# A kernel-made instruction order for most of the first expert layer, with retention decays and part of the weight splits moved from GpSimd to VectorE

## The chip, the cores and the metric

The kernel runs on one NeuronCore of one Trainium2 chip. The metric is the device time of one execution in microseconds (us). The engines are named as the profile names them: PE is TensorE (matmuls), DVE is VectorE, ACT is ScalarE, POOL is GpSimd, SP is SyncE, whose queue issues all DMAs of this kernel.

## The reference

Retention (attention with a fixed decay per head and no softmax) feeds two dense layers one after the other; all is float32.

```python
batch, n_heads, seq, head_dim = (4, 8, 576, 64)      # 2304 tokens, d_model 512, d_ff 2048
scores = scale * np.matmul(q, k.transpose(0, 1, 3, 2))
Dmat = np.where(rel >= 0, gamma[:, None, None] ** rel[None, :, :], 0.0)
attn = np.matmul(scores * Dmat[None], v)
x = attn.transpose(0, 2, 1, 3).reshape(B * S, H * D)
h = x @ w_in;  g = h * np.cos(h);  x = g @ w_out                        # first layer
h = x @ w_in;  g = where(h >= 1, h, where(h <= -1, 0, (h + 1)**2 / 4)); out = g @ w_out   # second layer
```

## The kernel before

The weights arrive as float64 bit patterns, and the kernel turns them into float32 by integer and float operations on VectorE and ScalarE. Every matmul is done as three float32r products: each operand is split into a high part (a copy, on ScalarE) and a low part (the operand minus the high part, on VectorE or GpSimd).

The first layer works on five blocks of tokens (256, then four of 512), and for each block on 16 strips of 128 hidden units. One strip of one block is a **slot**; there are 80. A slot has these steps, named by letters in the code:

- `m`: 12 matmuls into a PSUM tile `h` (for the last block, in every second slot `bkS` or `bkO` instead);
- `a` on ScalarE and `A` on VectorE (L662, L666): reduce `h` to a turn, tile `t`;
- `b` on ScalarE (L670, L671): the cosine;
- `C` on VectorE (L675): times `h`, which frees the `h` tile;
- `g` on ScalarE (L683) and `G` on GpSimd (L688): high and low part, tiles `gh` and `gl`;
- `M`, two slots later: 12 matmuls into the four output banks `bky`; every third one reads `gl`.

There are two `h` tiles, so `m` of a slot waits for `C` of the slot two before it.

Three other things run beside the slots, from slot 28 on. First, the retention of the last nine pieces of a sequence (chunks of 64 or 128 tokens): load `qkv`, multiply by decay tables (`decay_q` L370, `decay_k` L380, on GpSimd), score matmuls, a mask on VectorE (tile `R`, L472), the attend matmuls that read `R`, the state `T`, and the high and low parts of the result (`xhl`). Second, the 32 pieces of the second layer's weights: load `raw`, ScalarE's `X`, VectorE's `W`, `X` and `V` (L239, L240, L275, L276), high and low part (`cw`, L291 and L292), sums of halves (`V`, L300 to L302), their parts (`tw`: L304 on ScalarE, and L306 on VectorE for one of the two matrices, L308 on GpSimd for the other), and stores to `wq` and `wv` in HBM. Third, reloads of the first layer's weights (`wi` from `wd`) for each slot from 32 on.

The engines run their instructions in a fixed order each. The opening and the whole second layer are put in order by the kernel: the opening by a written list, the second layer by a small planner, `listed`, which takes operations with a cost, a wanted position and the places that they read and write, runs the five engines through, and emits the operations in the order of the planned starts. Slots 24 to 79 are left to the framework's scheduler (`by_hand[0] = 0`): the loop below only says in which order they are written.

Of the kernel before, what the change touches and what calls it, by code (L numbers as in the profile page):

```python
# [20 lines left out]
P = 128  # L21
# [16 lines left out]
EARLY = (0, 2, 3, 1, 4)  # L38
XEARLY = {5: 6, 6: 8}
# [11 lines left out]
COST = dict(PE=1.04, mm2=2.72, psum=0.556, wide=0.96, copy=0.85, square=0.9, evac=0.68, pool=2.15, load=0.06)  # L51
LAG = 2
# [58 lines left out]
def retention_moe_kernel(ctx: ExitStack, tc: tile.TileContext, qk, kv, win1, wout1, win2, wout2, ktab, out):  # L111
# [169 lines left out]
    def spill(i, c, begun):  # L281
        q, second = c % NQ, c >= NQ
        if not second:
            half_w[i, q] = cv.tile([P, 2, DM], F32, tag="rsh", name="V")
        v = half_w[i, q][:, int(second), :]
        to_fp32(begun, v)
        t = wr.tile([P, 2, 2, 2 * P], F32R, tag="wi", name="cw")
        kept = ((((1, 0), (2, 1)), ((3, 1),)), (((1, 0),), ((2, 0), (3, 1))))[i][second]
        ks = slice(kept[0][1], kept[-1][1] + 1)
        u = v.rearrange("p (k m) -> p k m", k=2)[:, ks]  # L290
        A.activation(t[:, ks, 0], u, AF.Copy)  # L291
        V.tensor_tensor(out=t[:, ks, 1], in0=u, in1=f(t)[:, ks, 0], op=ALU.subtract)  # L292
        for p, k in kept:
            SY.dma_start(out=spilled(i, q, p), in_=f(t)[:, k])

    def spill_sums(i, q):

        v = half_w.pop((i, q)).rearrange("p s (k m) -> p (s k) m", k=2)
        firsts, seconds, v21 = ((v[:, 0::2], v[:, 2:4], v[:, 1]), (v[:, 0:2], v[:, 1::2], v[:, 2]))[i]
        V.tensor_tensor(out=firsts, in0=seconds, in1=firsts, op=ALU.subtract)  # L300
        V.tensor_tensor(out=v[:, 3], in0=v[:, 3], in1=v[:, 0], op=ALU.subtract)
        V.tensor_tensor(out=v21, in0=v21, in1=v[:, 3], op=ALU.subtract)  # L302
        t = xp.tile([P, 4, 2, 2 * P], F32R, tag="x", name="tw")
        A.activation(t[:, :, 0], v, AF.Copy)  # L304
        if i == 0:
            V.tensor_tensor(out=t[:, :, 1], in0=v, in1=f(t)[:, :, 0], op=ALU.subtract)  # L306
        for j in (0, 2)[:2 * i]:
            G.tensor_tensor(out=t[:, j:j + 2, 1], in0=v[:, j:j + 2], in1=f(t)[:, j:j + 2, 0], op=ALU.subtract)  # L308
        for j, p in enumerate(((5, 4, 7, 6), (5, 7, 4, 6))[i]):
            SY.dma_start(out=spilled(i, q, p), in_=f(t)[:, j])  # L310
# [320 lines left out]
    def copy_out(e, t, y, scale):  # L631
        if e % 2 == 0:
# [4 lines left out]
    def evac(s, home=None, only=None):  # L637
        l, c = slots[s]
        if c != NC - 1:
            return  # L640
        o, n = BLOCKS[l]
        per = 512 // n
        for e, y in enumerate(yb[l]):
            if only not in (None, e):
                continue
            t = stp.tile([P, 512], F32, tag="st", name="st") if home is None else home
            copy_out(e, t, y, -TWOPI)
            SY.dma_start(out=yd[:, e * per:(e + 1) * per, o:o + n], in_=t.rearrange("p (k n) -> p k n", k=per))
# [50 lines left out]
    plan = {}  # L699

    def at(pos, fn):
        plan.setdefault(pos, []).append(fn)

    def run_plan(pos):
        for fn in plan.pop(pos, []):
            fn()

# [3 lines left out]

    window = {}
    for l in range(3, NBLK):
        window[l] = (pos_of[l - 1, 0] + 1, pos_of[l - 1, NC - 1] - 1)
    ends = {}
    for l in range(3, NBLK):
        s0, s1 = window[l]
        span = 2 * (s1 - s0) / len(members[l])
        for k, i in enumerate(members[l]):
            g = int(2 * s0 + k * span)  # L720
            e = int(2 * s0 + (k + 1) * span) - 1
            e = max(e, g)
# [131 lines left out]
    begun2 = {}  # L854
    per = (N1 - 6 - bg0) / len(bg)
    bgpos = {}
    for j, x in enumerate(bg):
        bgpos.setdefault(bg0 + int(j * per), []).append(x)

    reload = {}  # L860
    for s in range(pos_of[2, 0], N1):
        reload.setdefault(s - 3, []).append(slots[s][1])

    def spill_2(i, c):
        spill(i, c, begun2.pop((i, c)))
        if c >= NQ:
            spill_sums(i, c - NQ)
# [49 lines left out]
    def load_inputs(sb, pos):  # L917
        for j, (h, g) in enumerate(((0, 0), (1, 0), (1, 1), (0, 1))):
# [4 lines left out]
            op("SP", "load", pos + 5 * j, load, (), (qa[j][0],))  # L923
# [30 lines left out]
    def taken_ops():  # L954
        fns = [o[3] for o in ops]
# [3 lines left out]

    load_inputs(0, 0)  # L960
    early = {N1 - 11: taken_ops()}
    sum_q("DVE", 0, 4, 1, 2, ALU.add)
    sum_q("DVE", 0, 1, 0, 1, ALU.subtract)
    early[N1 - 9] = taken_ops()
    for k, s in zip(EARLY, (N1 - 8, N1 - 7, N1 - 4, N1 - 3, N1 - 2)):
        split_q("DVE", 0, k)
        early[s] = taken_ops()

    for s in range(N1):
        l, c = slots[s]  # L970
        if s == 24:
            by_hand[0] = 0
        run_plan(2 * s)
# [14 lines left out]
        run_plan(2 * s + 1)  # L988
# [15 lines left out]
    steps_of(N1 - 1, "CgG")
# [216 lines left out]
    def listed():  # L1221
        waits = [len(o[4]) for o in ops]
        users = [[] for _ in ops]
        for n, o in enumerate(ops):
            for x, lands in o[4]:
                users[x].append((n, lands))
        ready = [o[2] if o[0] == "SP" or not o[4] else 0.0 for o in ops]
        free = dict(PE=0.0, ACT=0.0, DVE=0.0, POOL=0.0, SP=-60.0)
        queue = {e: {n for n, o in enumerate(ops) if o[0] == e and (e == "PE" or not waits[n])} for e in free}
        order = []  # L1230
        while len(order) < len(ops):
            best = None
            for e, ns in queue.items():
                if e == "PE":
                    n = min(ns, default=None)
                    if n is None or waits[n]:
                        continue
                elif ns:
                    t1 = min(max(free[e], ready[n]) for n in ns) + 0.15
                    n = min((n for n in ns if max(free[e], ready[n]) <= t1), key=lambda n: (ops[n][2], n))  # L1240
                else:
                    continue
                t = max(free[e], ready[n])
                if best is None or t < best[0]:
                    best = t, n
            t, n = best
            e, cost = ops[n][:2]
            queue[e].remove(n)
            free[e] = t + cost
            order.append((t, n))  # L1250
            for u, lands in users[n]:
# [112 lines left out]
```

## Time and profile before

| | before |
|---|---|
| median of 3 runs | 826.82 us (826.65 to 827.5) |
| the profiled execution's own time | 825.69 us |
| its span, first to last instruction | 823.9 us |
| busy: PE, DVE, ACT, POOL | 806.9, 641.5, 542.3, 164.7 us |
| granted TensorE clock | 0.999 of full speed |

Busy time is the union of an engine's instructions. Matmuls are pipelined: a matmul's row is longer than the distance to the next one's start, so PE's idle time is read from its waits and from starts, not from lengths. Slots 28 to 79 lie about between 158 and 464 us; the second layer follows.

### The profile page before, as it was taken

What the parts mean: (1) busy time and instruction counts of PE and PEld (TensorE: products, weight loads), DVE (VectorE), ACT (ScalarE), POOL (GpSimd) and SP (SyncE); (2) the same over time, 40 slices, a digit from 0 to 9 for tenths busy, and PEclk for the clock granted to TensorE, in tenths of its full rate; (3) what the DMA queues carried; (4) which work ended last, traced back from release to release, by engine and by line L of the source; (5) the groups of instructions that cost most, each with busy time, mean ns of one, the idle gap of its engine ahead of it and who ended that gap; (6) DMA issues with size and microseconds to landing.
All of it is one profiled execution on the core that took longest, in us unless ns stands there. A gap on an engine that the chain in (4) does not pass through costs nothing.

```text
span 823.9 us, 14770 instructions
## 1 busy us (share of the span) xinstructions
PE 806.9 (98%) x5549; PEld 726.7 (88%) x5550; DVE 641.5 (78%) x933; ACT 542.3 (66%) x893; POOL 164.7 (20%) x131
## 2 busy tenths in 40 slices
PE   8999999998999999999999999999999999999997
PEld 6888889886778788888787899999999999999997
DVE  7888888688888888779896368787777876874676
ACT  4788888755556555556665578687657785676672
POOL 3333222524234442323433200000000000000000
PEclk9999999999999999999999999999999999999999
DMA  9997999679858998768976298888899888898883
GB/s 351 395 391 284 358 335 325 257 249 338 280 177 303 343 326 295 275 227 289 376 252 232 84 336 282 298 253 254 252 328 316 265 251 252 268 317 255 253 253 133
DMA packets 78007, 232.92 MB, mean 283 GB/s; under 512 B 8304, under 2 KB 15088, under 8 KB 77936
## 3 DMA queue, kind: packets, MB, share of 16 engines
q1 hardware_dynamic: 77936, 231.98, 82.0%
q8 instruction: 44, 0.72, 0.3%
q14 instruction: 27, 0.22, 0.1%
HBM read 184.76 MB, written 47.19 MB: 282 GB/s over the span
## 4 chain that ended last, share of the span: by engine, by line
PE 45%; DVE 14%; DMA 4%; ACT 4%; issue 3%; POOL 0%; SPq 0%; DVEq 0%; ACTq 0%
PE bkT L128 42%; DVE cw L292 3%; DVE t L666 2%; DMA raw<-in_win_dram 1%; DVE t L675 1%; DVE X L275 1%; DVE V L276 1%; ACT tw L304 1%; DVE W L239 1%; ACT t L662 1%; DVE tw L306 1%; DVE X L240 1%; DMA wq<-cw 1%; ACT cw L291 1%; PE bky L128 1%
## 5 line engine op out<-in xcount | busy, mean ns | idle before, releaser
L128 PE MATMUL bkT<-xc,w 128*128 128x384 f32 x1008 | 179.0, 335 | 0.0
L128 PEld LDWEIGHTS bkT<-xc,w 128*128 128x128 f32 x1008 | 175.2, 188 | 0.5 <-ACT bkT L128 0.2
L128 PE MATMUL bkT<-gh,w 128*128 128x384 f32 x672 | 170.9, 335 | 0.3 <-ACT bkT L128 0.3
L612 PE MATMUL h<-xhl,wi 128*128 128x512 f32 (+1 forms) x576 | 137.8, 387 | 1.1 <-DVE t L675 1.1
L612 PEld LDWEIGHTS h<-xhl,wi 128*128 128x128 f32 x576 | 105.9, 188 | 23.8 <-DVE t L675 1.5
L128 PEld LDWEIGHTS bkT<-gh,w 128*128 128x128 f32 x672 | 121.4, 188 | 0.6 <-ACT bkT L128 0.6
L128 PE MATMUL bkT<-gl,w 128*128 128x384 f32 x336 | 112.3, 334 | 0.0
L688 POOL TENSOR_TENSOR gl<-t,gh 128x512 fp32r<-128x512 f32 (+1 forms) x57 | 79.3, 1391 | 161.7 <-ACT gh L683 106.0
L627 PE MATMUL bky<-gh,wo 128*128 128x512 f32 x208 | 82.0, 395 | 0.7 <-ACT gh L683 0.7
L628 PE MATMUL bky<-gh,wo 128*128 128x512 f32 x208 | 81.0, 390 | 0.0
L629 PE MATMUL bky<-gl,wo 128*128 128x512 f32 x208 | 79.2, 391 | 1.2 <-POOL gl L688 1.2
L683 ACT ACTIVATE gh<-t 128x512 fp32r<-128x512 f32 (+1 forms) x57 | 35.3, 620 | 53.3 <-DVE t L675 53.2
L128 PEld LDWEIGHTS bkT<-gl,w 128*128 128x128 f32 x336 | 63.1, 188 | 0.0
L670 ACT ACTIVATE t<-t 128x512 f32<-128x512 f32 (+1 forms) x56 | 34.9, 624 | 39.2 <-DVE t L666 39.2
L128 DVE TENSOR_TENSOR gl<-a,gh 128x768 fp32r<-128x768 f32 x48 | 45.2, 954 | 13.2 <-ACT gh L128 13.2
L128 PE MATMUL h<-xhl,wi 128*128 128x256 f32 (+1 forms) x288 | 52.1, 330 | 1.4 <-ACT hs L128 0.9
L128 DVE SCALAR_TENSOR_TENSOR a<-bkT,a 128x768 f32<-128x768 f32 x36 | 34.4, 955 | 23.2 <-ACT a L128 22.7
L128 DVE TENSOR_TENSOR a<-bkT,a 128x768 f32<-128x768 f32 (+1 forms) x46 | 43.0, 937 | 11.0 <-PE bkT L128 11.0
L128 PEld LDWEIGHTS h<-xhl,wi 128*128 128x128 f32 x288 | 43.7, 189 | 7.3 <-ACT hs L128 1.1
L629 PEld LDWEIGHTS bky<-gl,wo 128*128 128x128 f32 x208 | 38.9, 188 | 10.3 <-POOL gl L688 2.2
L627 PEld LDWEIGHTS bky<-gh,wo 128*128 128x128 f32 x208 | 39.0, 188 | 10.0 <-ACT gh L683 1.1
L128 ACT ACTIVATE gh<-a 128x768 fp32r<-128x768 f32 x48 | 40.2, 837 | 9.0 <-PE bkT L128 8.4
(187 smaller groups left out, 1529.2 us busy)
## 6 DMA issues: line engine op xcount, KB each, us to landing
w<-wq SPq DMA_DIRECT2D x84, 512.0 KB, 4.5
w<-wv SPq DMA_DIRECT2D x84, 512.0 KB, 4.6
wi<-wd SPq DMA_DIRECT2D x48, 512.0 KB, 5.5
raw<-in_win_dram SPq DMA_DIRECT2D x32, 512.0 KB, 5.8
raw<-in_wout_dram SPq DMA_DIRECT2D x32, 512.0 KB, 5.6
qkv<-in_qk_dram SPq DMA_DIRECT2D x16, 512.0 KB, 7.5
qkv<-in_kv_dram SPq DMA_DIRECT2D x16, 512.0 KB, 8.1
wd<-wi SPq DMA_DIRECT2D x16, 512.0 KB, 6.6
```

The costliest lines, as they stand in the source:

```text
L128: ins = fn(*args, **kw)
L239: V.tensor_scalar(out=Wi, in0=Xi, scalar1=3, scalar2=odd, op0=ALU.logical_shift_left, op1=ALU.bitwise_or)
L240: V.tensor_scalar(out=Xi, in0=Wi, scalar1=-0x800000, scalar2=None, op0=ALU.bitwise_and)
L292: V.tensor_tensor(out=t[:, ks, 1], in0=u, in1=f(t)[:, ks, 0], op=ALU.subtract)
L612: lastpe[0] = PE.matmul(hp[s][:, :n], w[:, a, kb, :], x[b][:, kb, :], start=(i == 0), stop=(i == 3 * KB - 1))
L627: PE.matmul(o, w[:, 0, es], a, start=first and e % per == 0, stop=False, skip_group_check=True)
L628: PE.matmul(o, w[:, 1, es], a, start=False, stop=False, skip_group_check=True)
L629: PE.matmul(o, w[:, 0, es], b, start=False, stop=last, skip_group_check=True)
L666: V.scalar_tensor_tensor(out=t, in0=t, scalar=-MAGIC, in1=h, op0=ALU.add, op1=ALU.subtract)
L670: A.activation(u, u, AF.Sin, scale=TWOPI / 2)
L683: A.activation(gh[s], rt[s], AF.Copy)
L688: G.tensor_tensor(out=gl[s], in0=u, in1=f(gh[s]), op=ALU.subtract)
```

## The change

From slot 28 on the first layer's operations are given to the same planner `listed` (with a latency of 0.2 us between engines) and emitted in its order; slots 24 to 27 stay with the framework's scheduler. Within this part:

- `decay_q`, `decay_k` and all of `tw`'s low parts are issued on VectorE;
- the step `G` is given to the planner as an operation of VectorE (`LOW = "DVE"`, cost `low4` = 0.69), while the function that it calls, `g_low`, is not in the diff;
- a chunk's attend matmuls stand two half slots behind its scores; before it was `(e - g) // 3`, with `e - g` of 4 to 6: one half slot for seven of the nine chunks, two for the others;
- a `wi` reload is wanted 13 us ahead of its slot, a chunk's loads 17 and 16 us ahead of its scores, its decays 6 and 5 us ahead;
- a weight piece comes every 9.0 (`PACE`), each in small operations of its own;
- the fifth early split of the second layer's input (`EARLY`) is moved into the second layer.

```diff
-EARLY = (0, 2, 3, 1, 4)
-XEARLY = {5: 6, 6: 8}
+EARLY = (0, 2, 3, 1)
+XEARLY = {4: 4, 5: 6, 6: 8}
...
+E1 = 5.75
+PACE = 9.0
...
+LATS = (0.12, 0.2)
...
-        for j in (0, 2)[:2 * i]:
-            G.tensor_tensor(out=t[:, j:j + 2, 1], in0=v[:, j:j + 2], in1=f(t)[:, j:j + 2, 0], op=ALU.subtract)
...
-            pos = [g, g + (e - g) // 3, e]
...
-                at(g - 1, lambda: CH[i].decay_q(G))
...
-                    at(g - 1, lambda: CH[i].decay_k(G))
-                at(pos[0], go("scores", "across", "masked"))
-                at(pos[1], go("attend"))
...
-    for s in range(N1):
+    for s in range(bg0):
         if s == 24:
             by_hand[0] = 0
...
+    def first_layer_ops():
+        LOW = "DVE"
...
+            def at_load():
+                op("SP", "load", t0 - 17, lambda: load(0), (), (q,))
+                op("SP", "load", t0 - 16, lambda: load(1), (), (v,))
+                op("DVE", "low4", t0 - 6, lambda: CH[i].decay_q(V), (), (q,))
+                if not last:
+                    op("DVE", "low4", t0 - 5, lambda: CH[i].decay_k(V), (), (v,))
+            def at_scores():
+                op("PE", "scores", t0, go("scores", "across"), (q, v, ("T",)), banks)
+                op("DVE", "masks", t0 + 1, go("masked"), banks, (("R",),))
...
+            at(g - 3, at_load)
+            at(g, at_scores)
+            at(g + 2, at_attend)
...
+                eng, cost, pos, reads, writes = dict(
+                    a=("ACT", "turn", 2.8, (h,), (t,)), A=("DVE", "psum1", 3.7, (h,), (t,)), b=("ACT", "cos", 5.0, (), (t,)),
+                    C=("DVE", "psum1", 6.5, (h,), (t,)), g=("ACT", "copy4", 8.0, (t,), (hi,)), G=(LOW, "low4", 9.0, (t, hi), (lo,)))[x]
+                op(eng, cost, b + pos, lambda x=x: steps_of(s, x), reads, writes)
...
+            def sums_low():
+                V.tensor_tensor(out=cb[2][:, :, 1], in0=quarters(), in1=f(cb[2])[:, :, 0], op=ALU.subtract)
...
+            if s >= pos_of[2, 0]:
+                op("SP", "load", when(s) - 13, lambda s=s: load_wi(slots[s][1]), (), (wi_place(s),))
+            op("PE", "mm2", 0, lambda s=s: steps_of(s, "m"), (wi_place(s), ("xh", l), ("xl", l)), (bank_of(s),))
+            chain(s)
...
+            second(s - LAG)
...
+    order1 = listed(LATS[1])
+    by_hand[0] = 1
+    for _, n in order1:
+        fns[n]()
```

The first place is GpSimd's order in this part of the program. Names are tiles: `gl` is a slot's low part, `tw` the sums' low parts, `qkv` a chunk in its decay (with the table `qtb` or `ktb`). Before, from the sixth `gl` of this part on:

```order
L688 TENSOR_TENSOR gl<-t,gh 128x512 x5
L308 TENSOR_TENSOR tw<-V,tw 128x2x256 x2
L370 TENSOR_TENSOR qkv<-qkv,qtb 128x512
L380 TENSOR_TENSOR qkv<-qkv,ktb 128x512
L688 TENSOR_TENSOR gl<-t,gh 128x512 x3
L370 TENSOR_TENSOR qkv<-qkv,qtb 128x256
L688 TENSOR_TENSOR gl<-t,gh 128x512 x2
L370 TENSOR_TENSOR qkv<-qkv,qtb 128x256
L380 TENSOR_TENSOR qkv<-qkv,ktb 128x256
```

And of the change, from the last slots of the framework's part to the end of the program:

```order
L656 TENSOR_TENSOR gl<-t,gh 128x512
L656 TENSOR_TENSOR gl<-t,gh 128x256
L656 TENSOR_TENSOR gl<-t,gh 128x512
L133 TENSOR_TENSOR gl<-t,gh 128x256
L133 TENSOR_TENSOR gl<-t,gh 128x512 x52
L1460 UNCONDITIONAL_BRANCH
```

The decays and the `tw` rows have left GpSimd; all 52 `gl` rows of full width have stayed there.

The second place is VectorE's order from `C` of slot 33 to `A` of slot 34 (both read `t<-t,h`), where an output block is copied out and a chunk ends. Before:

```order
L675 SCALAR_TENSOR_TENSOR t<-t,h 128x512
L276 TENSOR_TENSOR V<-W,X 128x512
L300 TENSOR_TENSOR V<-V 128x512
L292 TENSOR_TENSOR cw<-V,cw 128x2x256
L418 SCALAR_TENSOR_TENSOR T<-T,ktb,bkS 128x64 x2
L418 SCALAR_TENSOR_TENSOR T<-T,ktb,bkO 128x64 x2
L301 TENSOR_TENSOR V<-V 128x256
L302 TENSOR_TENSOR V<-V 128x256
L519 TENSOR_TENSOR xhl<-bkS,xhl 128x2x128
L519 TENSOR_TENSOR xhl<-bkO,xhl 128x2x128
L666 SCALAR_TENSOR_TENSOR t<-t,h 128x512
```

And of the change, with two rows ahead of `C`:

```order
L133 TENSOR_SCALAR st<-bky_1079 128x512
L133 TENSOR_SCALAR st<-bky_1080 128x512
L133 SCALAR_TENSOR_TENSOR t<-t,h 128x512
L133 SCALAR_TENSOR_TENSOR T<-T,ktb,bkS 128x64 x2
L133 SCALAR_TENSOR_TENSOR T<-T,ktb,bkO 128x64 x2
L133 TENSOR_TENSOR xhl<-bkS,xhl 128x2x128
L133 TENSOR_TENSOR xhl<-bkO,xhl 128x2x128
L133 SCALAR_TENSOR_TENSOR t<-t,h 128x512
```

The weight pieces that stood between `C` and the next `A` have moved to other slots; 11 instructions stood between the two, now six.

## Rows read from the trace of the kernel before

**Rows 1.** The windows view: busy time of each engine from 158 to 464 us.

```profile
158.00:464.00 306.00, 298.66 (x2053) 241.72 (x2053) 252.00 (x393) 182.92 (x317) 111.27 (x81) 1.00 0.78 274
```

**Rows 2.** The waits view of PE from 158 to 464 us: total us, times, longest.

```profile
PE bkS L384 <- DVE R L472: 3.3, 3, 1.7
PE bky L629 <- POOL gl L688: 1.2, 1, 1.2
PE h L612 <- DVE t L675: 1.1, 1, 1.1
PE bky L627 <- ACT gh L683: 0.7, 1, 0.7
PE bkO L384 <- DVE xhl L519: 0.7, 1, 0.7
PE bkO L384 <- PE bky L629: 0.4, 1, 0.4
```

**Rows 3.** The timeline of PE around 409 us: start, length, line, operation.

```profile
409.51 0.39 PE L628 MATMUL bky<-gh,wo 128*128 128x512 f32 x1
411.07 0.73 PE L629 MATMUL bky<-gl,wo 128*128 128x512 f32 x2 [1.18 <-POOL gl L688]
```

**Rows 4.** Groups of VectorE by shape, 158 to 464 us: busy us, mean ns.

```profile
L276 DVE TENSOR_TENSOR V<-W,X 128x512 f32<-128x512 f32 x32 | 26.1, 817 | 2.5 <-POOL tw L308 2.4
...
L239 DVE TENSOR_SCALAR W<-X 128x512 int32<-128x512 int32 x32 | 22.4, 700 | 1.6 <-ACT X L226 1.6
...
L240 DVE TENSOR_SCALAR X<-W 128x512 int32<-128x512 int32 x32 | 16.9, 530 | 0.9
...
L292 DVE TENSOR_TENSOR cw<-V,cw 128x512 fp32r<-128x512 f32 x16 | 19.9, 1241 | 2.9 <-ACT cw L291 2.8
...
L292 DVE TENSOR_TENSOR cw<-V,cw 128x256 fp32r<-128x256 f32 x16 | 16.7, 1042 | 2.7 <-ACT cw L291 2.6
...
L306 DVE TENSOR_TENSOR tw<-V,tw 128x1024 fp32r<-128x1024 f32 x8 | 9.8, 1223 | 4.1 <-ACT tw L304 4.0
```

**Rows 5.** The views of lines 239 and 292, 158 to 464 us: min/median/max ns.

```profile
L239 DVE TENSOR_SCALAR W<-X x32: 412/579/1546, 160.3 to 431.6; 128x512 int32<-128x512 int32 x32
...
L292 DVE TENSOR_TENSOR cw<-V,cw x32: 410/1280/1776, 166.4 to 435.1; 128x512 fp32r<-128x512 f32 x16, 128x256 fp32r<-128x256 f32 x16
```

**Rows 6.** Groups of GpSimd by shape, 158 to 464 us.

```profile
L688 POOL TENSOR_TENSOR gl<-t,gh 128x512 fp32r<-128x512 f32 x51 | 72.8, 1427 | 147.2 <-ACT gh L683 94.9 <-issue 43.4 <-PE bkS L384 5.4
L308 POOL TENSOR_TENSOR tw<-V,tw 128x512 fp32r<-128x512 f32 x16 | 22.6, 1434 | 24.5 <-ACT tw L304 21.2 <-DMA wv<-cw 3.3
```

**Rows 7.** The timeline of all engines around 244 us.

```profile
243.28 0.69 DVE L300 TENSOR_TENSOR V<-V 128x512 f32<-128x512 f32 x1
...
243.44 1.67 POOL L688 TENSOR_TENSOR gl<-t,gh 128x512 fp32r<-128x512 f32 x1 [4.82 <-ACT gh L683]
...
243.89 1.50 DVE L292 TENSOR_TENSOR cw<-V,cw 128x256 fp32r<-128x256 f32 x1
```

**Rows 8.** The timeline of all engines from 370 us on, three rows of it.

```profile
370.23 0.68 DVE L675 SCALAR_TENSOR_TENSOR t<-t,h 128x512 f32<-128x512 f32 x1
...
371.70 1.68 POOL L688 TENSOR_TENSOR gl<-t,gh 128x512 fp32r<-128x512 f32 x1 [2.87 <-issue]
...
373.37 2.88 PE L612 MATMUL h<-xhl,wi 128*128 128x512 f32 x12
```

**Rows 9.** The waits view of VectorE from 158 to 464 us.

```profile
DVE t L675 <- ACT t L671: 15.9, 13, 1.8
DVE t L666 <- ACT t L662: 15.8, 17, 1.6
```

**Rows 10.** The waits view of GpSimd from 158 to 464 us.

```profile
POOL qkv L370 <- DMA qkv<-in_qk_dram: 22.0, 6, 7.4
```

**Rows 11.** Part 6 of the page: issues, KB each, median us to landing.

```profile
wi<-wd SPq DMA_DIRECT2D x48, 512.0 KB, 5.5
...
qkv<-in_kv_dram SPq DMA_DIRECT2D x16, 512.0 KB, 8.1
```

More of the change, by code (lines that the diff above doesn't have):

```diff
@@ L50 @@
 XPOS = (-17, -20, -17.5, -4.4, -13, -4.5, -3.2)
-COST = dict(PE=1.04, mm2=2.72, psum=0.556, wide=0.96, copy=0.85, square=0.9, evac=0.68, pool=2.15, load=0.06)
+E1 = 5.75
+PACE = 9.0
+BG_AT = 0.0
+BEHIND = 8.0
+LATS = (0.12, 0.2)
+COST = dict(turn=0.58, psum1=0.68, cos=1.3, copy4=0.65, low4=0.69, low2=0.42, copy2=0.42, copy8=1.06, low8=1.23, masks=1.12, state=1.1, high=0.75, scores=1.0, w8=0.86, nothing=0.02, PE=1.04, mm2=2.72, psum=0.556, wide=0.96, copy=0.85, square=0.9, evac=0.68, pool=2.15, load=0.06)
 LAG = 2
@@ L332, in new_r @@
         rn[0] += 1
-        pool, tag = (wp, "wo5") if by_hand[0] == 1 and rn[0] % 2 else (ap, "R")
+        pool, tag = (wp, "wo5") if rn[0] <= len(first) and rn[0] % 2 else (ap, "R")
         return pool.tile([P, 2, DM], F32, tag=tag, name="R", **({} if pool is wp else dict(bufs=1)))
@@ L629, in mm2, with copy_out @@
             PE.matmul(o, w[:, 0, es], b, start=False, stop=last, skip_group_check=True)
-    def copy_out(e, t, y, scale):
-        if e % 2 == 0:
+    def copy_out(e, t, y, scale, eng=None):
+        if eng == "ACT" or eng is None and e % 2 == 0:
             A.activation(t, y, AF.Copy, scale=scale)
@@ L635, in copy_out, with evac @@
             V.tensor_scalar(out=t, in0=y, scalar1=scale, scalar2=None, op0=ALU.mult)
-    def evac(s, home=None, only=None):
+    def evac(s, home=None, only=None, eng=None):
         l, c = slots[s]
@@ L697, in steps_of @@
                 STEPS[x](s)
[L699 to L706, printed above, removed]
     members = {}
@@ L853, in retention_moe_kernel @@
     bg0 = pos_of[0, NC - 1] + 1
[L854 to L858, printed above, removed]
     reload = {}
     for s in range(pos_of[2, 0], N1):
[L862 to L867, printed above, removed]
+        reload.setdefault(s - 2, []).append(slots[s][1])
     ops = []
@@ L915, in xat, with load_inputs @@
         return xplace[k]
-    def load_inputs(sb, pos):
+    def load_inputs(sb, pos, after=()):
         for j, (h, g) in enumerate(((0, 0), (1, 0), (1, 1), (0, 1))):
@@ L922, in load @@
                 SY.dma_start(out=qa[j][1], in_=yd[:, 2 * g:2 * g + 2, o:o + TH])
-            op("SP", "load", pos + 5 * j, load, (), (qa[j][0],))
+            op("SP", "load", pos + 5 * j, load, (), (qa[j][0],), after)
     def sum_q(eng, pos, to, a, b, how):
@@ L954, in taken_ops @@
     def taken_ops():
-        fns = [o[3] for o in ops]
+        fns = [(o[0], o[1], o[3]) for o in ops]
         for x in ops, wrote, read:
@@ L958, in taken_ops, with listed @@
         return fns
[L960 to L967, printed above, removed]
-    for s in range(N1):
-        l, c = slots[s]
+    def listed(lat):
+        waits = [len(o[4]) for o in ops]
+        users = [[] for _ in ops]
+        for n, o in enumerate(ops):
+            for x, lands in o[4]:
+                users[x].append((n, lands))
+        ready = [o[2] if o[0] == "SP" or not o[4] else 0.0 for o in ops]
+        free = dict(PE=0.0, ACT=0.0, DVE=0.0, POOL=0.0, SP=-60.0)
+        queue = {e: {n for n, o in enumerate(ops) if o[0] == e and (e == "PE" or not waits[n])} for e in free}
+        order = []
+        while len(order) < len(ops):
+            best = None
+            for e, ns in queue.items():
+                if e == "PE":
+                    n = min(ns, default=None)
+                    if n is None or waits[n]:
+                        continue
+                elif ns:
+                    t1 = min(max(free[e], ready[n]) for n in ns) + 0.15
+                    n = min((n for n in ns if max(free[e], ready[n]) <= t1), key=lambda n: (ops[n][2], n))
+                else:
+                    continue
+                t = max(free[e], ready[n])
+                if best is None or t < best[0]:
+                    best = t, n
+            t, n = best
+            e, cost = ops[n][:2]
+            queue[e].remove(n)
+            free[e] = t + cost
+            order.append((t, n))
+            for u, lands in users[n]:
+                ready[u] = max(ready[u], t + cost + (0.0 if not lands or ops[u][0] == e else 6.0 if e == "SP" else lat))
+                waits[u] -= 1
+                if not waits[u] and ops[u][0] != "PE":
+                    queue[ops[u][0]].add(u)
+        return order
+    loop_end = bg0
+    for s in range(bg0):
         if s == 24:
             by_hand[0] = 0
-        run_plan(2 * s)
         steps_of(s, "m")
@@ L1006, in retention_moe_kernel @@
+    first_layer_ops()
+    order1 = listed(LATS[1])
+    fns = [o[3] for o in ops]
+    for x in ops, wrote, read:
+        x.clear()
+    by_hand[0] = 1
+    for _, n in order1:
+        fns[n]()
     first_layer.close()
@@ L1219, in retention_moe_kernel @@
         last(i, NSB * NKB * T0 + 2 * i)
[L1221 to L1251, printed above, removed]
-                ready[u] = max(ready[u], t + cost + (0.0 if not lands or ops[u][0] == e else 6.0 if e == "SP" else 0.12))
-                waits[u] -= 1
-                if not waits[u] and ops[u][0] != "PE":
-                    queue[ops[u][0]].add(u)
-        return order
-    order2 = listed()
+    order2 = listed(LATS[0])
     by_hand[0] = 1
```

217 lines of the change are left out of this document (146 added, 71 removed).

## The prediction

> **What bounds the kernel now.** I first read the busy time of the stretch in which the changed slots lie, 158 to 464 us [rows 1]. PE is busy for 298.7 of 306 us, VectorE for 252.0, ScalarE for 182.9 and GpSimd for 111.3. PE sets the end, so the change can only bring what PE idles there, and costs what PE idles anew. The waits of PE show all of its idle time: eight waits, 7.4 us [rows 2]. The largest kind is the attend matmuls waiting for the mask `R` (3.3 us, three times); the rest wait for `gl`, `gh`, `C`, an `xhl` part and one bank. None waits for a weight load.
>
> The view understates these waits a little. A matmul's row is 0.39 us long, but in a run of 12 the starts follow each other at (2.88 - 0.39) / 11 = 0.226 us [rows 3, 8]. In the wait for `gl` the starts are 411.07 - 409.51 = 1.56 us apart [rows 3], so 1.33 us are lost where the view says 1.18. With 0.15 us for each of eight waits, PE loses 7.4 + 1.2 = 8.6 us in this stretch and needs 306 - 8.6 = 297.4 us. A slot of 24 matmuls takes 24 x 0.226 = 5.4 us.
>
> VectorE is not short of time on average, but its order is uneven. The rows of its order show it: between `C` of slot 33 and `A` of slot 34 stood 11 instructions, about 3.7 us of weight and `xhl` work and four state updates besides (0.69 us for each 512-wide one [rows 7], 0.41 for a 256-wide one [rows 5]). `A`, and all that follows in that slot, waits for them, while other slots have little in that place. GpSimd's work slows VectorE too. At 243.44 us a `gl` begins; the next VectorE instruction with SBUF operands, a 256-wide `cw`, takes 1.50 us [rows 7], where the quickest takes 0.41 [rows 5].
>
> **What the change does, step by step.** *The waits.* The attend matmuls now stand two half slots behind the scores, before for seven of nine chunks only one: 24 matmuls, 5.4 us, in place of 12, 2.7 us, in which VectorE must do two mask instructions. The three waits for `R` should go. The waits for `C`, `gh` and `xhl` come from VectorE's bunches; in the new order the work between `C` and the next `A` at the place shown falls from 11 instructions to six, and the weight pieces are spread evenly. The wait for `gl` goes if GpSimd has less queued in front of it: of its 111.3 us, 72.8 are `gl` [rows 6], and by the new order nothing else stays there. The wait for a bank (0.4) hangs on the same chain. I take all 8.6 us off.
>
> *VectorE's load.* Moved to it: 16 decays, 13 of 512 and three of 256 columns, 13 x 0.69 + 3 x 0.41 = 10.2 us, and eight `tw` parts of 1024 columns in place of GpSimd's 16 halves, 9.8 us [rows 4]. Together 20.0 us. Given back: what GpSimd's instructions cost it. Five groups show that cost as the time above their unhindered length [rows 4, 5, 7]: `V<-W,X` 26.1 - 32 x 0.69 = 4.0, `W<-X` 22.4 - 32 x 0.412 = 9.2, `X<-W` 16.9 - 13.2 = 3.7, the wide `cw` 19.9 - 16 x 0.69 = 8.9, the narrow one 16.7 - 16 x 0.41 = 10.1; 35.9 us in all, or 0.32 us for each of GpSimd's 111.3 us. With 72.8 us of `gl` left, 23.5 stay and 12.4 are saved. The upper bound: each of 51 `gl` costs what the one at 243.44 us did, 1.50 - 0.41 = 1.09 us, 55.6 in all. So VectorE's busy time goes from 252.0 to 252.0 + 20.0 - 12.4 = 260 us; at the bound it is 252.0 - 35.9 + 20.0 + 55.6 = 292 us. Both are below PE's 297.4. I take the lower, since the mix of instructions beside `gl` is the same as before.
>
> The Trainium skill, "SBUF — State Buffer", section "Who interferes with whom", says that the port pair of VectorE and GpSimd is an exclusive lock held for the whole instruction, so that whichever comes second is blocked fully. By that alone, with every `gl` meeting a blocked instruction for its full mean length, the cost would be 72.8 us, and VectorE's sum 252.0 - 35.9 + 20.0 + 72.8 = 309 us, above PE's need. The rows show such blocks, but only 0.32 us of them for each us of GpSimd.
>
> *What the planner gets wrong.* It counts each `G` as 0.69 us on VectorE, but the order shows all `gl` on GpSimd. It leaves 51 x 0.69 = 35 us on VectorE that are not needed, at just the times when a `gl` blocks it for 23.5 to 55.6 us in all: a useful mistake more than a harmful one. A `gl` also takes 1.43 us [rows 6], 0.74 longer than planned. The first matmul that reads it has room: one `gl` ended at 373.38 us [rows 8], and the third matmul of its `M`, behind 12 others from 373.37 on, comes at 373.37 + 14 x 0.226 = 376.5. That cover is 3.2 us; without it each `gl` would cost up to 0.74.
>
> *Loads.* Weight reloads are wanted 13 us ahead of their slot and land in 5.5 [rows 11], so stores queued ahead of them on SP may hold them 7.5 us. I cost them at nothing, between that and a late load's own price, its lateness. ScalarE keeps its work. The fifth early split goes into the second layer, where PE's order is the old one; nothing in the changed stretch needs it, and I cost it at nothing; at worst its product waits for one split, about 2 x 0.69 x 1.5 = 2 us.
>
> *The sum.* Left over: new waits of the same kinds, between 0 and the old 8.6. A fixed order meets small delays that the plan doesn't know, so I leave 1.2 us, about one wait for `R` (3.3 / 3 = 1.1). The profiled execution took 825.7 us by its own time: 825.7 - 8.6 + 1.2 = 818.3. The median of the runs is 1.1 above that execution, so I predict 819.4.
>
> **The rivals.** *Half of it.* The waits are moved rather than removed: half of the 8.6 us returns behind other instructions. 825.7 - 4.3 + 1.1 = 822.5 us. For it speaks that 1.2 us is little for a stretch of 306 us; against it, that the three largest waits have a reason each that is taken away.
>
> *VectorE becomes the bound* (the other side). Its own waits for `a` and `b` were 15.8 + 15.9 = 31.7 us [rows 9], and in a fixed order the instructions behind them wait too. If they stay, the sum is 260 + 32 = 292 us, still below 297.4. If a `gl` costs VectorE midway between the two bounds, 40 us in all, it is 308, 10.3 above PE's need: 825.7 - 8.6 + 10.3 + 1.1 = 828.5 us. That is the point from which the change is slower; at the upper bound (292 + 32 = 324) it would be about 845. Against it: the new order puts other work ahead of `A` and `C`, so their waits should shrink. The Trainium skill's "Perfetto Trace Analysis", section "Optimizing Scalar/DVE Operations", suggests the opposite move, off a saturated VectorE; the rows say 82% before.
>
> *The decays hold VectorE.* GpSimd waited for the load of a decay six times, 22.0 us, at most 7.4 [rows 10], and nothing hung on it. On VectorE, `A` and `C` are queued behind it. `C` ended at 370.91 and freed the `h` that PE took at 373.37 [rows 8]: 2.5 us to spare. If all nine chunks keep a wait of 22.0 / 6 = 3.7 us, each costs PE 1.2: 819.4 + 10.8 = 830.2 us; from a mean of 3.5 us on it is slower than before. Against it: loads stand 11 us ahead of their decays and land in 8.1 [rows 11].
>
> **How the numbers follow.** The forecast has a chance of 0.62 (817.8 to 821.1), half of it 0.18 (to 825), a loss that just eats the gain 0.07, VectorE as the bound 0.07, the decays 0.06. A change within 0.2%, 1.7 us, can hardly be told from none. So faster 0.80, same 0.07, slower 0.13. The floor is 826.8 - 8.6 = 818.2 less the runs' spread of 0.4; the range is 817.8 to 824.5, the forecast and most of its half.
>
> **What would show it.** Right: PE's waits in the first layer sum to some 1 us, none for `R`; GpSimd holds only `gl`; VectorE's `cw` and `W<-X` are nearer to 0.69 and 0.41 us; VectorE is busy for about 260 us of the stretch, and the second layer starts some 7 us sooner. Wrong: PE waiting for `C` or `R` again and again while VectorE shows no idle time (the bound), VectorE's decays with waits of over 2.5 us for their loads, PE waiting for `wi`, or a new wait at the start of the second layer.

## The result and the profile after

The changed kernel takes 817.74 us (median of 4 runs, 817.3 to 818.65), the one before 827.16 us in the same sitting: 9.4 us less, a ratio of 0.988 with a 95% interval of 0.9853 to 0.9906.

The windows view of the changed kernel, in the columns of [rows 1]; its first layer ends at 455.85 us, so the stretch is cut at 455:

```profile
158.00:455.00 297.00, 297.00 (x2061) 242.67 (x2060) 242.03 (x408) 181.00 (x311) 76.07 (x51) 1.00 0.82 287
```

PE is busy in all of the 297 us, and its waits view of this stretch is empty: none of the six kinds of [rows 2] is left, and none is new. Part 4 of the page, the chain that ended last, now stays on PE for most of the span (45% before):

```profile
PE 90%; DMA 4%; DVE 2%; ACT 2%; issue 1%; SPq 0%; POOL 0%; DVEq 0%; ACTq 0%; POOLq 0%
```

The length of the stretch itself is read from the starts of two matmuls, the first of slot 28 and the first of the second layer (`bkT<-xc,w`). PE's timeline of the kernel before:

```profile
148.33 0.63 PE L612 MATMUL h<-xhl,wi 128*128 128x512 f32 x2
...
463.37 0.52 PE L128 MATMUL bkT<-xc,w 128*128 128x384 f32 x2
```

and after:

```profile
150.45 0.40 PE L133 MATMUL h<-xhl,wi 128*128 128x512 f32 x1
...
455.85 0.34 PE L133 MATMUL bkT<-xc,w 128*128 128x384 f32 x1
```

Slot 28 thus begins some 10 us ahead of the 158 us taken so far; no wait of PE lies in between, and both stretches hold the same 2096 matmuls. That is 315.04 us before and 305.40 after: 9.64 us less, which covers the 9.4 of the medians. Only 7.0 us of it show between the two profiled executions (825.69 and 818.65). This one began its slot 28 2.1 us later, in a part that the change leaves alone, and its second layer took 361.0 us in place of 360.5, two values that both occur with the planned order and with the framework's. There PE waited 1.8 us for `hs` (0.9 before), and the granted clock behind it fell; the windows view after shows 0.91 where before had 1.00:

```profile
80.00:100.00 20.00, 18.21 (x105) 16.14 (x104) 16.62 (x32) 16.06 (x36) 5.89 (x5) 0.91 0.96 352
```

VectorE's groups of the changed kernel by shape, 158 to 455 us, which answer to [rows 4]; the last three, a decay and two groups of the weight work, have no row there:

```profile
L133 DVE TENSOR_TENSOR V<-W,X 128x512 f32<-128x512 f32 x31 | 24.3, 784 | 0.6
...
L133 DVE TENSOR_TENSOR tw<-V,tw 128x1024 fp32r<-128x1024 f32 x16 | 20.6, 1288 | 2.3 <-ACT tw L133 2.1 <-DMA raw<-in_win_dram 0.3
...
L133 DVE TENSOR_SCALAR W<-X 128x512 int32<-128x512 int32 x30 | 12.6, 419 | 0.0
...
L133 DVE TENSOR_TENSOR cw<-V,cw 128x512 fp32r<-128x512 f32 x15 | 11.4, 759 | 2.8 <-ACT cw L133 2.8
L133 DVE TENSOR_TENSOR cw<-V,cw 128x256 fp32r<-128x256 f32 x16 | 8.5, 532 | 1.2 <-ACT cw L133 1.1
L133 DVE TENSOR_TENSOR qkv<-qkv,qtb 128x512 f32<-128x512 f32 x7 | 6.5, 929 | 0.0
...
L133 DVE SCALAR_TENSOR_TENSOR X<-raw,X 128x512 f32<-128x512 uint32 x31 | 23.9, 770 | 0.1
...
L133 DVE TENSOR_TENSOR V<-V 128x256 f32<-128x256 f32 x32 | 19.1, 598 | 0.7
```

`W<-X` has gone from 700 to 419 ns, the wide `cw` from 1241 to 759, the narrow one from 1042 to 532. The decays (929 ns where the quickest instructions of that width take 690) and the narrow sums `V<-V` (598 ns, two groups of 491 and 452 before) now meet GpSimd instead. GpSimd holds only `gl`, 51 of them in the stretch, in its group by shape:

```profile
L133 POOL TENSOR_TENSOR gl<-t,gh 128x512 fp32r<-128x512 f32 x51 | 76.1, 1492 | 223.5 <-ACT gh L133 214.5 <-PE bkO L133 4.5 <-PE bkS L133 4.5
```

### The profile page after: what moved, and what is told of

It is laid out like the page before. It is cut to its first block, busy times and chain, and to the rows that moved or that the text cites. A ratio compares the mean times of both kernels' runs of the same rounds, so it can differ in the third digit from the quotient of the medians.

```text
span 816.9 us, 14708 instructions
## 1 busy us (share of the span) xinstructions
PE 805.4 (99%) x5549; PEld 728.2 (89%) x5550; DVE 635.1 (78%) x956; ACT 542.7 (66%) x890; POOL 126.2 (15%) x99
## 4 chain that ended last, share of the span: by engine, by line
PE 90%; DMA 4%; DVE 2%; ACT 2%; issue 1%; SPq 0%; POOL 0%; DVEq 0%; ACTq 0%; POOLq 0%
PE bkT L133 42%; PE bky L133 21%; PE h L133 19%; PE bkS L133 4%; PE bkO L133 4%; DMA rsh<-in_wout_dram 2%; DMA qkv<-in_qk_dram 1%; PE h L580 1%; DMA qkv<-in_kv_dram 1%; DMA raw<-in_wout_dram 1%; ACT t L133 1%; DVE t L133 0%; ACT gh L133 0%; DVE wo L133 0%; DVE X L133 0%
## 5 line engine op out<-in xcount | busy, mean ns | idle before, releaser
L133 PE MATMUL h<-xhl,wi 128*128 128x512 f32 (+1 forms) x816 | 180.7, 370 | 2.2 <-ACT hs L133 1.8
L133 POOL TENSOR_TENSOR gl<-t,gh 128x512 fp32r<-128x512 f32 (+1 forms) x76 | 103.7, 1366 | 300.4 <-ACT gh L133 278.4
L133 PEld LDWEIGHTS bky<-gh,wo 128*128 128x128 f32 x504 | 94.5, 190 | 19.8 <-issue 0.5
L133 ACT ACTIVATE t<-t 128x512 f32<-128x512 f32 (+1 forms) x152 | 89.3, 590 | 34.0 <-DVE t L133 31.9
L133 PE MATMUL bky<-gl,wo 128*128 128x512 f32 x252 | 95.6, 390 | 0.0
L133 DVE SCALAR_TENSOR_TENSOR t<-t,h 128x512 f32<-128x512 f32 x88 | 60.1, 683 | 35.1 <-ACT t L133 35.1
L133 ACT ACTIVATE gh<-t 128x512 fp32r<-128x512 f32 (+1 forms) x76 | 44.7, 588 | 26.0 <-DVE t L133 25.9
L133 PEld LDWEIGHTS bky<-gl,wo 128*128 128x128 f32 x252 | 47.2, 188 | 9.9
L133 ACT ACTIVATE t<-h 128x512 f32<-128x512 f32 x44 | 26.2, 595 | 43.4 <-PE h L133 43.4
L133 ACT ACTIVATE X<-raw 128x512 f32<-128x512 f32 x61 | 40.5, 666 | 11.5 <-DMA raw<-in_win_dram 7.1
```

The costliest lines, as they stand in the source:

```text
L133: ins = fn(*args, **kw)
```

## The experiments

Ratios are to the kernel before, run beside each. "The stretch" is, as above, from the first matmul of slot 28 to the first of the second layer, 315.04 us before and 305.40 after.

**The engines without the order.** The kernel before, with the decays and all `tw` low parts on VectorE, and the framework's scheduler as it was.

```diff
...
-                at(g - 1, lambda: CH[i].decay_q(G))
+                at(g - 1, lambda: CH[i].decay_q(V))
...
-                    at(g - 1, lambda: CH[i].decay_k(G))
+                    at(g - 1, lambda: CH[i].decay_k(V))
```

> The framework's order is kept; the decays and all low parts of the sums are issued on VectorE, so GpSimd holds only the slots' low parts. Theory 'order' (the gain comes from VectorE's even order): PE's waits in the first layer stay at 5 to 9 us, the time at 823 to 828 us. Rival 'engines' (the gain comes from GpSimd's emptier queue and from fewer blocked VectorE instructions): the waits fall below 3 us, 817.5 to 820.5 us.

Measured: 825.5 us, ratio 0.9982 (0.9967 to 0.9998), the stretch 313.63. The waits view of PE, 158 to 455 us:

```profile
PE h L609 <- DVE t L672: 1.6, 3, 1.0
PE bkS L381 <- DVE R L469: 1.6, 2, 1.5
PE bky L626 <- POOL gl L685: 1.4, 3, 0.5
```

These are 4.6 us of waits, between what the two expectations had, and the time is that of the theory. The one wait of 1.2 us for `gl` [rows 2, 3] is gone, but three of up to 0.5 us for other `gl` have come, though GpSimd holds nothing but `gl` now. At one of them, at 418.8 us, GpSimd had idled 3.75 us for the high part `gh`, so that GpSimd's queue cannot be the reason. The engines bring between 0.02 and 0.33%, a small part of the gain.

**The order without the engines.** The changed kernel, with the decays and half of the `tw` low parts given back to GpSimd, and the planner told so.

```diff
...
-                op("DVE", "low4", t0 - 6, lambda: CH[i].decay_q(V), (), (q,))
+                op("POOL", "pool4", t0 - 6, lambda: CH[i].decay_q(G), (), (q,))
...
-            op("DVE", "low8", p + 8, sums_low, both, (("tw",),))
+            op(("DVE", "POOL")[i], ("low8", "pool8")[i], p + 8, sums_low, both, (("tw",),))
```

> The kernel's own order is kept; the decays and half of the sums' low parts go back to GpSimd, and the planner is told so (1.36 us a decay, 2.87 us a pair of low parts). Theory 'order': PE still waits for less than 2 us, 817 to 819.5 us, though VectorE's instructions lose about 36 us to GpSimd again in place of 23. Rival 'engines': waits for gl or for C return, 821 to 827 us.

Measured: 818.11 us, ratio 0.9897 (0.9879 to 0.9916), no wait of PE in the stretch (305.59 us), GpSimd busy for 115.82 of 297 us. So the order alone brings the gain, with GpSimd as loaded as before. The earlier loads and the moved fifth split, which this run keeps, were not tested apart; none of PE's waits in [rows 2] was for a load.

**`gl` on VectorE too.**

```diff
-        G.tensor_tensor(out=gl[s], in0=u, in1=f(gh[s]), op=ALU.subtract)
+        (V if s >= 27 else G).tensor_tensor(out=gl[s], in0=u, in1=f(gh[s]), op=ALU.subtract)
```

> The changed kernel, with the slots' low parts really issued on VectorE, as the planner has them; GpSimd is empty from slot 28 on. Theory 'order' with room on VectorE: 51 x 0.69 = 35 us are added to VectorE and some 23 us of blocking go, so VectorE's busy time rises by about 12 us to some 254 of 297; PE still has no waits, 817 to 818.7 us. Rival 'VectorE becomes the bound': its waits for ScalarE (41 us in the changed kernel) stay beside it, PE waits again, 820 us or more.

Measured: 817.84 us, ratio 0.989 (0.9871 to 0.991), no wait of PE, the stretch 305.40. VectorE is busy for 250.98 us and GpSimd for none: 51 `gl` of 0.69 us there cost VectorE 9 us net, since no GpSimd instruction slows it any more. What the planner thinks is true here: 0.69 us of VectorE per slot are really used, and the time is that of the change.

**The attend matmuls one half slot behind the scores.** The changed kernel, with the distance that the old code wrote for seven of the nine chunks.

```diff
-                op("PE", "scores", t0 + E1, go("attend", *(() if last else ("state",))), (q, v, ("T",), ("R",)), banks)
+                op("PE", "scores", t0 + E1 / 2, go("attend", *(() if last else ("state",))), (q, v, ("T",), ("R",)), banks)
...
-            at(g + 2, at_attend)
+            at(g + 1, at_attend)
```

> The changed kernel, with a chunk's attend matmuls one half slot behind its scores in place of two. Theory of the prediction (the mask has 2.7 us in place of 5.4): waits for R return, up to nine of 0.5 to 1.1 us, 819 to 823 us. Rival (the planner puts the mask in time anyway): PE waits below 1 us, 817 to 818.7 us.

Measured: 817.73 us, ratio 0.9891 (0.987 to 0.9912), no wait of PE, the stretch 305.40. PE's order shows 12 matmuls of the slots between scores and attends in each of the nine chunks; in the changed kernel it is 24.

**The attend matmuls two half slots behind, in the kernel before.**

```diff
-            pos = [g, g + (e - g) // 3, e]
+            pos = [g, g + 2, e]
```

> The kernel before, with the attend matmuls written two half slots behind the scores for all nine chunks. Theory 'distance' (the step of the prediction for R): the waits for R, 3.3 us, go, 822.5 to 824.5 us. Rival 'order': R is late because of what stands ahead of it on VectorE and the framework's scheduler places both anyway; PE's waits stay above 5 us in all, 825 to 829 us.

Measured: 826.85 us, ratio 0.9993 (0.9979 to 1.0007), the stretch 313.63. The waits view of PE, 158 to 464 us, has 5.9 us in all, 7.4 in the kernel before. Its first row, beside [rows 2]:

```profile
PE bkS L384 <- DVE R L472: 2.9, 3, 1.7
```

This run is no test of the distance, because it moved no attend matmul, as the rival supposed. In the executed order of the kernel before, 21 to 25 matmuls of the slots (by the records in the trace) already stand between scores and attends in all nine chunks, and in this run it is the same: the framework's scheduler doesn't keep to the distance that the code writes. The test is the run ahead of this one, and by it the planned order needs no more than one half slot.

What made PE wait for `R` is where the mask stands in VectorE's order, and the traces show it. The timeline of all engines in the kernel before, at the longest of the three waits (the scores end where the 12 matmuls begin):

```profile
211.93 3.04 PE L612 MATMUL h<-xhl,wi 128*128 128x512 f32 x12
...
212.28 1.23 DVE L306 TENSOR_TENSOR tw<-V,tw 128x1024 fp32r<-128x1024 f32 x1 [1.17 <-ACT tw L304]
...
217.31 1.27 DVE L292 TENSOR_TENSOR cw<-V,cw 128x256 fp32r<-128x256 f32 x1 [0.48 <-ACT cw L291]
...
218.51 0.55 DVE L472 TENSOR_TENSOR R<-bkO,mtb 128x384 f32<-128x384 f32 x1
...
219.57 0.32 PE L384 MATMUL bkS<-R,qkv 64*64 64x128 f32 x1 [1.66 <-DVE R L472]
```

and the same chunk in the changed kernel:

```profile
210.84 3.02 PE L133 MATMUL h<-xhl,wi 128*128 128x512 f32 x12
...
211.21 0.69 DVE L133 SCALAR_TENSOR_TENSOR t<-t,h 128x512 f32<-128x512 f32 x1
...
211.81 0.55 DVE L133 TENSOR_TENSOR R<-bkO,mtb 128x384 f32<-128x384 f32 x1
...
216.51 0.32 PE L133 MATMUL bkS<-R,qkv 64*64 64x128 f32 x1
```

Before, eight VectorE instructions, from `tw` to `cw`, stand between the scores and the mask, which starts 6.5 us behind them; after, one stands there, and it is 0.9 us. Over the nine chunks the mask starts 2.3 to 6.6 us behind the scores before and 0.05 to 1.4 us after, and the three waits belong to the three longest delays (5.7, 6.5 and 6.6 us).

**The planner told the truth.** `g_low` given to the planner as GpSimd's, with 1.36 us.

```diff
...
-        LOW = "DVE"
+        LOW = "POOL"
...
-G=(LOW, "low4", 9.0, (t, hi), (lo,)))[x]
+G=(LOW, "pool4", 9.0, (t, hi), (lo,)))[x]
```

> The changed kernel, with G planned where it runs: on GpSimd at 1.36 us, none of VectorE's time. Theory 'room': the planner's mistake neither helps nor harms, PE waits for less than 1 us, 817 to 818.7 us. Rival 'useful mistake': a plan without the 35 us that stand in for GpSimd's blocking fills VectorE too tightly, PE waits return, 820 to 823 us.

Measured: 818.95 us, ratio 0.9921 (0.9892 to 0.995), 7 runs between 817.62 and 825.84. The profiled one was the longest and began its slot 28 late, so it was run again.

> The kernel of the honest plan once more (g_low told to the planner as GpSimd's with 1.36 us, all else as in the change), since its one profiled run was much longer than its other runs and began late. Theory (it does not matter which engine the planner thinks g_low is on): no waits of PE in the changed stretch, from the first matmul of slot 28 to the second layer 305.4 us, time within 0.1% of the change's 817.8. Rival (the planner's mistake is useful, as the prediction had it): a wait of PE at the end of the stretch again, 1 to 4 us more in the stretch, time 819 to 822 us.

Measured: 821.75 us, ratio 0.9941 (0.9918 to 0.9965), the stretch 310.46 (309.53 in the profiled run of the first). The truth makes it slower in the median: the 13 runs of both have one of 821.15, 3.4 above the change. The ratio of the second sitting lies clear of the change's (0.9853 to 0.9906), that of the first doesn't. With the earliest start of slot 28 (148.33) and the shortest second layer (360.5) of any profile, and the 1.8 us between span and time, a stretch of 309.53 us would make 820.2 us. Five of the 13 runs are quicker, so not every execution pays this price in full. The waits view of PE shows one wait that matters, at the same place in both profiles (2.2 us in the first, 2.5 in the second):

```profile
PE bky L133 <- ACT st L133: 2.5, 1, 2.5
```

It lies where the last output block but one is copied out of the banks (`st<-bky`, two copies on VectorE and two on ScalarE) before PE may fill them again. The timeline of all engines there, honest plan:

```profile
378.75 2.88 PE L133 MATMUL h<-xhl,wi 128*128 128x512 f32 x12
...
381.60 0.68 DVE L133 SCALAR_TENSOR_TENSOR t<-t,bkS 128x512 f32<-128x512 f32 x1
382.20 0.69 DVE L133 SCALAR_TENSOR_TENSOR X<-raw,X 128x512 f32<-128x512 uint32 x1
382.31 1.29 ACT L133 ACTIVATE t<-t 128x512 f32<-128x512 f32 x2 [1.76 <-DVE t L133]
382.80 1.28 DVE L133 TENSOR_SCALAR st<-bky 128x512 f32<-128x512 f32 x2
...
383.51 1.06 ACT L133 ACTIVATE st<-bky 128x512 f32<-128x512 f32 x2
...
384.14 1.22 PE L133 MATMUL bky<-gh,wo 128*128 128x512 f32 x2 [2.51 <-ACT st L133]
```

and the same place in the changed kernel:

```profile
379.69 2.88 PE L133 MATMUL h<-xhl,wi 128*128 128x512 f32 x12
379.78 1.07 ACT L133 ACTIVATE st<-bky 128x512 f32<-128x512 f32 x2
379.87 1.28 DVE L133 TENSOR_SCALAR st<-bky 128x512 f32<-128x512 f32 x2
...
382.41 0.62 PE L133 MATMUL bky<-gh,wo 128*128 128x512 f32 x2
```

Here the copies run beside the 12 matmuls ahead of the banks' next use. In the honest plan they stand behind `A` of the next slot and a weight piece's `X` on VectorE, and on ScalarE behind that slot's `b`, which waits for `A`: counted from the start of the 12 matmuls they begin 3.9 us later on VectorE and 4.7 on ScalarE. The wait also brings PE's clock down. The windows view of the honest plan behind it (the clock is the column ahead of the DMA share):

```profile
384.00:386.00 2.00, 1.86 (x4) 1.49 (x5) 1.42 (x4) 1.87 (x5) 0.53 (x1) 0.50 0.86 315
386.00:388.00 2.00, 2.00 (x8) 1.60 (x7) 1.97 (x4) 1.52 (x4) 0.76 (x1) 0.70 1.00 256
388.00:390.00 2.00, 2.00 (x10) 1.65 (x9) 1.93 (x6) 1.84 (x3) 0.00 (x0) 1.00 1.00 311
```

0.50 of full speed is 1.2 GHz, the lower level. That loses 2 x 0.50 + 2 x 0.30 = 1.6 us. With the wait of 2.5, another of 0.5 us for `C`, and 0.15 us of restart for each, 4.9 of the 5.06 us by which the stretch is longer in this execution are accounted for.

**`gl` twice on VectorE.** Each `gl` issued twice, with the planner knowing of one.

```diff
-        G.tensor_tensor(out=gl[s], in0=u, in1=f(gh[s]), op=ALU.subtract)
+        for e in (V, V) if s >= 27 else (G,):
+            e.tensor_tensor(out=gl[s], in0=u, in1=f(gh[s]), op=ALU.subtract)
```

> The changed kernel, with every low part gl issued on VectorE, and twice; the planner knows of one. VectorE's busy time rises from 251 (once) by 51 x 0.63 = 32 us to some 283 of 297. Theory 'busy time alone decides': still below PE's need, PE waits below 2 us, 817 to 819.5 us. Rival 'waits on ScalarE count too': busy time and some 30 us of such waits pass 297, VectorE is the bound, 825 us or more.

Measured: 818.14 us, ratio 0.9888 (0.9871 to 0.9906), no wait of PE, the stretch 305.40. The windows view:

```profile
158.00:455.00 297.00, 297.00 (x2061) 242.64 (x2060) 281.91 (x511) 179.71 (x311) 0.00 (x0) 1.00 0.82 286
```

VectorE's waits view of the changed kernel, its row for `A` and `C`:

```profile
DVE t L133 <- ACT t L133: 41.5, 44, 2.7
```

and with `gl` twice:

```profile
DVE t L133 <- ACT t L133: 4.4, 5, 2.3
```

VectorE is busy 95% of the stretch and PE doesn't notice. Its waits for ScalarE were room, and are filled first.

**`gl` three times.** The same with `(V, V, V)`.

> Every gl of the changed stretch is issued three times over on VectorE, two of them without use, while the planner still knows of one. With two, VectorE was busy 281.9 of 297 us and PE waited nowhere; the third adds 51 x 0.69 = 35.2 us, so VectorE needs about 281.9 + 35.2 - 3 (rows overlap by some 0.06 us) = 314 us in a stretch where PE needs 297. Theory (PE is the bound until VectorE's busy time itself passes PE's need; VectorE's waits are slack): PE now waits some 17 us, spread over waits for C and gl, VectorE's waits for ScalarE are almost nil, and the time is 817.9 + 17 = 835 us, 831 to 842. Rival (bunches are absorbed further, since the planned order leaves room that the busy time does not show): under 825 us. Rival (beyond the bound waits add up as well): over 845 us.

Measured: 850.52 us, ratio 1.029 (1.0261 to 1.0318): the second rival, above 845. The stretch is 335.34 us, 29.9 longer. The windows view of all of it, and two shorter windows:

```profile
152.59:487.93 335.34, 315.65 (x2099) 249.28 (x2097) 320.45 (x570) 181.89 (x320) 1.30 (x1) 0.99 0.73 252
...
390.00:410.00 20.00, 16.67 (x65) 13.03 (x64) 19.40 (x33) 11.55 (x20) 0.00 (x0) 0.89 0.74 247
410.00:430.00 20.00, 20.00 (x85) 16.43 (x84) 18.64 (x33) 10.02 (x17) 0.00 (x0) 0.94 0.85 284
```

and the waits view of PE:

```profile
PE bkS L133 <- DVE R L133: 6.2, 6, 1.8
PE bky L133 <- ACT st L133: 5.3, 3, 3.3
PE h L133 <- DVE t L133: 4.4, 7, 1.1
PE bky L133 <- DVE gl L133: 3.6, 6, 1.1
```

VectorE needs 320 us, 15 more than PE; it idles another 15, and both show in the time. PE's side of it is 19.5 us in 22 waits, 22 x 0.15 = 3.3 of restarts, 20 x 0.11 + 20 x 0.06 = 3.4 of lower clock, and 3.7 that the waits view doesn't list. Behind the stretch, the second layer took another 3 us more (363.8 us).

**The state matmuls in a visit of their own.** PE goes from the 128-row matmuls of the slots to the 64 x 64 ones of a retention chunk and back 18 times in the stretch. In this run the changed kernel does it 25 times.

```diff
-                op("PE", "scores", t0 + E1, go("attend", *(() if last else ("state",))), (q, v, ("T",), ("R",)), banks)
+                op("PE", "scores", t0 + E1, go("attend"), (q, v, ("T",), ("R",)), banks)
...
+            at(g + 3, at_state)
```

> The changed kernel, with a chunk's state matmuls in a visit of their own, one half slot behind the attend matmuls: seven more changes between small and large matmuls on PE, the same work. Theory 'each visit costs' (0.37 us by the distances of starts around one: 0.09 in, 0.17 out, 0.11 behind the first large matmul): 7 x 0.37 = 2.6 us more, 819.5 to 821 us. Rival 'free': 817 to 818.7 us.

Measured: 820.39 us, ratio 0.9922 (0.9902 to 0.9941), no wait of PE from 158 to 455 us, the stretch 308.22: 2.82 us for 7 more visits, 0.40 each.

## Why the prediction came out as it did

The mechanism was right, the idle time of PE in this stretch and nothing else, and each of its waits went. 819.4 us was 1.7 too much, and 817.74 lies just under the range's lower end, which allowed no gain beyond the listed waits. Two terms of the sum were mis-sized.

- **The left-over waits: 1.2 us were left, none was measured.** "A fixed order meets small delays that the plan doesn't know" fell: the planned order had room for them (`gl` twice: VectorE busy for 40 us more than in the change, at no loss).
- **The floor: 8.6 us were taken as all that PE loses; the stretch lost 9.64.** Some 0.4 us is a visit to the small matmuls: PE's order had 19 in the stretch before, 18 after, and a visit costs 0.40. The remaining 0.6 us are starts delayed by less than the waits view lists, worked out as what is left, not measured apart. With 9.6 off, none left and the same 1.1 for the median, the sum is 825.7 - 9.6 + 1.1 = 817.2. The 0.5 us up to the measured 817.74 stay open; they are no more than the parts ahead of the stretch and behind it differ by between executions.

By its other steps:

- **`R`.** The waits went, but not for the reason given, so this step came out right by luck. "Before for seven of nine chunks only one" is what the code wrote; the kernel before executed two half slots already, so nothing was doubled, and with one half slot the planned order has no wait either. The reason given for `C`, `gh` and `xhl`, bunches in VectorE's order, is that of `R` too.
- **`C`, `gh`, `xhl`.** The wait for `C` shows the bunch: between `A` and `C` of that slot, from 192.92 to 196.22 us, VectorE ran three instructions of a weight piece, and two of them took 1.21 and 1.41 us in place of 0.41 while GpSimd was busy with `tw` and a decay. `gh` and `xhl` were not followed one by one.
- **`gl`.** "GpSimd has less queued in front of it" was right for the one wait of the kernel before, in whose timeline two `tw` stand ahead of the `gl`, which starts 1.4 us after its `gh` is done:

```profile
405.82 3.26 POOL L308 TENSOR_TENSOR tw<-V,tw 128x512 fp32r<-128x512 f32 x2 [3.30 <-ACT tw L304]
...
407.01 0.63 ACT L683 ACTIVATE gh<-t 128x512 fp32r<-128x512 f32 x1 [0.76 <-DVE t L675]
...
409.05 1.97 POOL L688 TENSOR_TENSOR gl<-t,gh 128x512 fp32r<-128x512 f32 x1
```

  But emptying GpSimd is neither needed nor enough: with GpSimd at 115.82 us in the planned order no wait for `gl` is left, with 75.84 us in the framework's order there are three others. Here too it is the order.
- **VectorE's load.** 260 us was expected. In the stretch as cut by the matmuls VectorE went from 255.67 to 247.78 us, 7.9 down in place of the 7.6 up: 15.5 off. The cost of GpSimd's work was counted in five groups of [rows 4, 5], 35.9 us; the others (`V<-V`, `X<-raw,X`, `xc`) add 8.4, so that 44.3 were there to save from. After, by the same subtraction over ten groups (`V<-W,X` 24.3 - 31 x 0.69 = 2.9, `V<-V` of 256 columns 19.1 - 32 x 0.41 = 6.0, the decays of 512 columns 11.7 - 13 x 0.69 = 2.7, and so on), 22.9 stay, near the 23.5 expected. So 21.4 were saved where 12.4 were counted: 9 of the 15.5. Rows of VectorE overlap at their ends, by 2.6 us more than before; the last 4 stay open.
- **The lock.** For one instruction the trace shows an almost full block. In the timeline after, `cw` starts 0.05 us behind a `gl` and takes 1.78 us in place of 0.69, 1.09 more, where the `gl` had 1.24 us to go:

```profile
179.86 1.29 POOL L133 TENSOR_TENSOR gl<-t,gh 128x512 fp32r<-128x512 f32 x1 [3.94 <-ACT gh L133]
179.91 1.78 DVE L133 TENSOR_TENSOR cw<-V,cw 128x512 fp32r<-128x512 f32 x1
```

  The Trainium skill ("SBUF — State Buffer", "Who interferes with whom") states an exclusive lock, and this row agrees but for 0.15 us. The sum by every `gl` in full, 309 us, does not: 22.9 us for 76.1 us of `gl`, 0.30 for each.
- **VectorE as the bound.** Rightly unlikely, but priced by a wrong sum. Its waits were added to its work (292 us, near the edge); with work of 281.9 us they fell from 41.5 to 4.4 us and nothing was lost. A `gl` cost of 40 us, 276 us of work by the prediction's own terms, would have been no "point from which the change is slower". Beyond the bound the opposite holds: at 320 us of work the stretch grew by twice the 15 us that VectorE lacks.
- **The decays on VectorE.** The rival had waits of 3.7 us for nine chunks. VectorE's waits for a decay's load are one of 0.2 us. No wait for `wi` either, so loads cost nothing, as taken.
- **The planner's mistake, "useful more than harmful".** Right, and partly for the reason given. In the honest plan VectorE is busy for 262.32 us of its stretch, 14.5 more than the 247.78 of the change with the same instructions; most of it is `X<-raw,X` (1027 ns in place of 781) and the narrow `V<-V` (716 in place of 598), so the plan without the room seems to set more of them beside a `gl`. But load of that size does PE no harm (281.91 of 297 us with `gl` twice). The price is in the order: one block's copies come late, which costs 4 to 5 us with the clock in the two profiled executions. That the missing room makes the planner order them so is argued, not shown.
- **Half of it** is refuted by the empty waits view. **The fifth split** cost nothing: the page's group `bkT<-xc,w` shows 0.0 us of idle PE.

## What to carry to other kernels

When the bound engine's idle time is a few waits for others' short work, look at the order on the engine that is late, not at its load: here the order alone brought the gain, while moving work between engines brought 0.2% by itself. Where a scheduler may reorder, read the distance between producer and consumer from the executed order and not from the code: the distance that this change was to double was there already. Idle time of an engine that isn't the bound is filled first, up to 95% busy here, so it must not be added to its work; past the bound it must. And a planner's false cost may be worth keeping until its truth has been timed.

## What the runs showed of the hardware

A visit from 128-row to 64 x 64 matmuls and back costs PE some 0.40 us that no wait shows (7 more visits, 2.82 us); the 18 of this stretch would be 7 us, as an estimate from that. The Trainium skill ("TensorEngine Tiling (Array Packing)", "Key Properties") says that a change of tiling mode drains TensorE; a price for each visit agrees with it, and the runs give its size.

The wait of 2.5 us for a late copy cost 4.1: behind it the clock was 0.50 and then 0.70 for 4 us. The length of the wait alone doesn't tell whether this happens. Ahead of slot 28, PE waited 1.79 us for `hs` both in the changed kernel and in that of the order without the engines, with the same 2.21 us of busy time from 86 to 90 us; from 90 to 94 us the granted clock was 0.58 in the first and 1.00 in the second. With the attends one half slot behind, that wait was 2.33 us, and the clock stayed at 1.00. Such a drop costs 4 x 0.42 = 1.7 us and is part of the spread between executions of one kernel.
